# Fewer warm-up matmuls, all at the start, and a new instruction order around them

## The chip, the core and the metric

The kernel runs on one core of a Trainium2 chip. The metric is the device time of one execution in microseconds. The engines are PE (TensorE), DVE (VectorE), ACT (ScalarE), POOL (GpSimd) and SP (SyncE, which here only issues DMAs); each takes its own instructions in order.

## The reference

Two blocks, each behind a layer norm that is modulated by a condition vector `c`, for 2048 tokens of width 512:

```python
mod = (silu(c) @ w_mod).reshape(1, 6, 1, 512)          # sa, ca, ga, sb, cb, gb
h = layernorm(x) * (1 + ca) + sa
x = x + ga * A(h)      # attention: 32 heads of 16, causal, a window of 256 tokens
h = layernorm(x) * (1 + cb) + sb
x = x + gb * B(h)      # layernorm again, then an MLP over the token axis:
                       # u = gelu(h^T @ w1 + b1), y = u @ w2 + b2, transposed back
```

`A` computes `qkv = h @ wqkv`, the scores of each query with the 256 keys up to its own position, their softmax, the weighted sum of the values and the product with `wo`. `w1` is 2048 x 1792, `w2` 1792 x 2048.

## The kernel before

Tokens stand in 16 tiles of 128. Four groups G of four tiles go through the first norm, the transpose (`h1T`, with the features on partitions), the projections to Q, K and V and the attention. Attention is cut into 75 chunks. Chunk i consists of S(i), a group of score matmuls of 32 rows each, four side by side, with 512 columns in each of four PSUM banks; two exps on ACT, a large one over three banks (`pss` to `et`, called EA) and a small one over the fourth (`psb` to `et`, EB); and a multiplication with the mask on DVE. Every few chunks the AV matmuls (`po`) follow, then ln and exp on ACT (`lz`, the reciprocal of the softmax sum) and a multiplication on DVE (`OT`). There is one three-bank tile `pss`, so S(i) waits until EA(i-1) has read it.

Between two score groups PE does other work: the projections of the next group (`pk`, `pq`, `pv`), the output projection (`pa`) of the last one, later the first half of the MLP's first product (`pu`, "partials", from w1 tiles `w1p` that SP loads). After the last chunk come the rest of `pu` and the second product `py`.

The opening (`proj0`, `opening`, lines 609 to 720) makes the first keys and queries. Warm matmuls on a zero tile (`warm`, lines 441 to 455) fill PE early: 16 matmuls of 128x512, two to an operation, into the `pss` tile. `silu` of c goes through a transpose on PE (`st`) and a copy on DVE (`sT`); 32 matmuls of one column (`fm`, output `ps_fm`) make the modulation of the first norm, copied by `fmc` to `modFM`. The first two token tiles are normalized (`xn`), transposed on PE (`tr`, output `psb`) and copied (`cp`) to `h1T`, which is then scaled and shifted with `modFM` (four operations `h1T`). Then come k, k, q, and another k and q, and S(0). The first k waits for `h1T` and for the warm matmuls, which use the same PSUM tile.

The order in which instructions stand on each engine is written out in the kernel. Every piece of work is an `Op`; `ORDER` (line 60) lists them all by number, `CHOSEN` (line 114) says which engine does those that several could do, and `run_schedule` (line 154) emits them in that order. A helper at line 234 keeps every emitted instruction in that program order, so in the profile all of them have line 234 (L234). The tail after the last `gg` operation is a plain loop over 16 output tiles.

Of the kernel before, what the change touches and what calls it, by code (L numbers as in the profile page):

```python
# [15 lines left out]
D = 512  # L16
# [41 lines left out]
E_BUFS = 7  # L58
LOG = None
ORDER = [  # L60
    2, 38, 3, 9, 40, 1, 10, 11, 4, 12, 41, 13, 14, 42, 16, 39, 8, 43, 44, 45, 17, 46, 18, 48, 47, 19, 6, 20, 7, 51,
    50, 49, 5, 52, 0, 53, 54, 56, 55, 57, 70, 58, 71, 126, 72, 75, 127, 73, 59, 76, 80, 60, 123, 81, 74, 128, 130,
    77, 61, 78, 82, 85, 131, 79, 86, 84, 83, 89, 63, 62, 132, 134, 87, 64, 124, 135, 65, 15, 67, 68, 66, 90, 88, 69,
    136, 138, 139, 264, 93, 121, 94, 129, 106, 91, 95, 142, 140, 96, 107, 265, 143, 98, 97, 92, 108, 266, 144, 166,
    111, 167, 267, 109, 99, 145, 268, 168, 100, 170, 112, 171, 110, 146, 133, 147, 113, 151, 137, 148, 174, 172,
    115, 152, 149, 173, 102, 175, 103, 150, 114, 141, 27, 104, 153, 269, 184, 176, 28, 494, 154, 156, 185, 271, 270,
    155, 157, 29, 116, 273, 177, 117, 272, 158, 188, 186, 118, 161, 159, 275, 120, 189, 495, 24, 119, 276, 187, 160,
    190, 198, 496, 101, 25, 199, 274, 724, 21, 22, 169, 162, 105, 200, 26, 202, 163, 23, 30, 203, 31, 497, 178, 191,
    498, 164, 206, 204, 179, 165, 32, 207, 180, 192, 193, 277, 194, 278, 181, 216, 208, 182, 279, 217, 183, 280,
    499, 36, 286, 281, 287, 218, 220, 282, 283, 195, 288, 221, 284, 209, 289, 292, 285, 222, 501, 725, 332, 196,  # L70
    293, 333, 290, 205, 298, 201, 299, 503, 294, 334, 336, 197, 295, 210, 291, 337, 37, 211, 34, 33, 212, 505, 125,
    500, 223, 314, 213, 340, 35, 338, 315, 300, 341, 956, 957, 219, 302, 310, 316, 311, 214, 335, 350, 296, 342,
    224, 312, 225, 351, 726, 226, 313, 301, 233, 215, 339, 352, 354, 504, 234, 727, 355, 297, 304, 235, 305, 728,
    356, 343, 364, 230, 227, 306, 365, 231, 357, 307, 317, 318, 232, 228, 368, 958, 366, 353, 344, 229, 369, 345,
    242, 122, 239, 319, 370, 308, 372, 236, 373, 371, 502, 237, 303, 243, 240, 374, 238, 506, 309, 382, 346, 383,
    241, 321, 320, 244, 322, 358, 384, 245, 386, 359, 347, 387, 323, 959, 246, 360, 375, 328, 348, 396, 388, 329,
    349, 508, 397, 324, 325, 330, 507, 361, 400, 729, 398, 367, 401, 516, 326, 247, 517, 399, 376, 518, 362, 404,
    402, 377, 389, 520, 519, 405, 513, 385, 363, 514, 731, 960, 248, 378, 406, 414, 249, 522, 515, 379, 415, 523,
    255, 327, 390, 391, 524, 380, 331, 732, 418, 416, 392, 381, 250, 419, 526, 509, 525, 510, 403, 521, 393, 407,
    428, 730, 420, 528, 511, 733, 429, 529, 408, 251, 734, 530, 430, 432, 417, 512, 540, 394, 256, 433, 531, 409,  # L80
    421, 541, 252, 410, 253, 434, 436, 411, 395, 437, 735, 542, 534, 257, 547, 527, 736, 412, 254, 446, 438, 548,
    543, 447, 413, 535, 961, 258, 422, 423, 536, 448, 450, 259, 439, 554, 451, 549, 555, 424, 537, 435, 452, 562,
    431, 544, 425, 556, 563, 545, 551, 546, 552, 532, 564, 566, 453, 440, 426, 261, 567, 738, 441, 442, 427, 538,
    449, 443, 737, 570, 568, 550, 454, 455, 444, 565, 571, 456, 445, 553, 463, 464, 533, 569, 457, 580, 572, 460,
    465, 260, 581, 461, 573, 739, 262, 462, 740, 458, 584, 582, 263, 459, 558, 472, 585, 466, 557, 583, 467, 741,
    586, 594, 468, 469, 595, 539, 473, 470, 758, 471, 596, 598, 559, 474, 599, 574, 475, 575, 600, 597, 602, 476,
    560, 576, 603, 759, 587, 743, 760, 744, 604, 612, 601, 577, 746, 613, 745, 747, 605, 588, 589, 477, 578, 748,
    616, 614, 749, 752, 617, 479, 615, 753, 579, 590, 478, 750, 962, 618, 626, 754, 762, 591, 481, 627, 480, 763,
    606, 742, 485, 592, 630, 755, 619, 628, 631, 482, 483, 486, 761, 632, 634, 593, 607, 487, 635, 608, 765, 484,
    751, 766, 609, 764, 963, 644, 636, 488, 645, 620, 621, 767, 622, 489, 633, 646, 648, 772, 610, 629, 561, 649,  # L90
    773, 611, 637, 784, 785, 647, 623, 774, 658, 650, 786, 659, 638, 491, 651, 769, 493, 770, 624, 662, 660, 639,
    771, 490, 663, 640, 625, 652, 492, 653, 654, 641, 768, 666, 664, 964, 642, 667, 965, 643, 966, 661, 665, 756,
    967, 668, 676, 969, 968, 655, 776, 677, 970, 669, 971, 757, 972, 678, 680, 670, 656, 681, 657, 671, 679, 672,
    973, 778, 673, 792, 974, 682, 779, 793, 683, 975, 976, 775, 977, 674, 796, 794, 978, 675, 780, 797, 684, 685,
    979, 782, 686, 795, 798, 800, 787, 690, 781, 687, 799, 801, 691, 693, 692, 694, 688, 810, 802, 788, 689, 695,
    811, 696, 803, 789, 697, 812, 790, 791, 814, 699, 815, 702, 980, 700, 703, 981, 816, 698, 824, 982, 701, 825,
    804, 813, 805, 704, 806, 826, 828, 817, 807, 986, 829, 705, 987, 983, 706, 988, 808, 984, 832, 830, 989, 833,
    809, 818, 831, 819, 827, 820, 990, 834, 842, 821, 991, 835, 843, 707, 992, 993, 777, 994, 844, 846, 822, 836,
    995, 847, 709, 837, 823, 838, 708, 783, 997, 848, 856, 710, 839, 711, 998, 857, 1002, 849, 1003, 712, 1004, 840,
    860, 858, 841, 999, 845, 861, 1005, 1000, 1008, 713, 862, 1001, 864, 1009, 865, 859, 714, 850, 1006, 851, 715,  # L100
    1007, 852, 866, 874, 863, 853, 1010, 875, 716, 1013, 1014, 1011, 854, 878, 876, 855, 1015, 867, 879, 1016, 1012,
    920, 717, 921, 880, 888, 1017, 1019, 922, 889, 1018, 923, 926, 1020, 924, 718, 890, 892, 996, 868, 881, 893,
    719, 869, 925, 870, 985, 1021, 927, 894, 896, 871, 1024, 897, 895, 1022, 891, 1025, 1023, 1026, 928, 720, 906,
    898, 929, 1030, 877, 907, 721, 1027, 899, 1031, 1028, 1032, 722, 872, 910, 908, 873, 882, 723, 883, 909, 911,
    884, 931, 930, 900, 901, 912, 933, 1033, 885, 1042, 1050, 886, 913, 1057, 1034, 932, 902, 914, 903, 915, 887,
    904, 916, 905, 1043, 917, 934, 1051, 918, 1058, 919, 935, 1071, 938, 936, 939, 1035, 940, 941, 942, 944, 1036,
    1064, 943, 1065, 1085, 945, 1037, 1078, 937, 946, 1038, 947, 1086, 1039, 948, 1072, 1052, 1040, 949, 1092, 951,
    1044, 1093, 950, 1029, 1087, 1066, 952, 1079, 1041, 1059, 953, 1094, 1080, 954, 955, 1073, 1045, 1046, 1067,
    1047, 1053, 1060, 1048, 1054, 1081, 1095, 1061, 1055, 1099, 1049, 1062, 1074, 1068, 1088, 1056, 1113, 1069,
    1075, 1100, 1106, 1063, 1076, 1082, 1107, 1108, 1089, 1083, 1109, 1120, 1077, 1070, 1127, 1096, 1101, 1090,  # L110
    1114, 1084, 1097, 1102, 1115, 1103, 1116, 1128, 1110, 1104, 1129, 1091, 1134, 1117, 1111, 1121, 1105, 1122,
    1098, 1123, 1118, 1135, 1124, 1136, 1112, 1130, 1125, 1119, 1137, 1131, 1138, 1132, 1139, 1133, 1126, 1140,
]
CHOSEN = {
    "ACT": [
        48, 50, 72, 74, 95, 1017, 1034, 1039,
    ],
    "DVE": [
        47, 49, 51, 52, 66, 69, 77, 79, 82, 84, 87, 91, 97, 100, 104, 108, 110, 113, 115, 118, 120, 248, 250, 252, 254,
        277, 278, 281, 285, 288, 294, 300, 306, 312, 316, 319, 323, 326, 330, 478, 480, 482, 484, 507, 508, 511, 515,  # L120
        518, 524, 530, 536, 542, 546, 549, 553, 556, 560, 708, 710, 737, 738, 741, 745, 748, 754, 760, 764, 767, 771,
        774, 780, 786, 790, 968, 973, 979, 984, 990, 995, 1001, 1006, 1012, 1023, 1028,
    ],
    "POOL": [
        712, 714,
    ],
}
BATCH = True
XT_AFTER = -0.7
W1_AFTER = 2.0  # L130
AV_POS = 0.2
LZ_POS = 0.0
M_POS = -0.5
# [60 lines left out]
def kernel(  # L194
# [116 lines left out]
    warm = modw.tile([P, D], BF, name="warm")  # L311
# [135 lines left out]
    def e_par(e):  # L447
        for par in range(2):
            ve.tensor_reduce(
                out=mask_par[:, par : par + 1], in_=ident_v[:, :, par, :], axis=mybir.AxisListType.XY, op=ALU.add,  # L450
            )

    parity = op("par", "DVE", 0.33, e_par, pos=-30, ready=2.2)
    warms = [op("warm", "PE", 0.86 if i < 4 else 0.43, lambda e, i=i: e_warm(e, 2, i == 0), pos=-7, cls="D", ready=1.4 if i < 4 else 4.8)
             for i in range(8)]

    def e_stps(e):
        box["st"] = bank([P, ND], BF, "st_ps")
# [3 lines left out]
            ready=2.8, pos=-20)  # L462
# [24 lines left out]
    fms = []  # L487
# [2 lines left out]
                      alloc=None if n else "od", ready=MOD_READY[n]))  # L490
    o_fm = op("fmc", "DVE", 0.25, e_fmc, deps=fms[-1:], pos=-12)
    fms[0].frees = [o_fm]


    def dense(name, pieces, emit, deps, pos, cls="D", alloc=None, ready=0.0):
# [858 lines left out]
```

## Time and profile before

| | |
|---|---|
| median of 3 runs | 257.99 us (256.64 to 258.8) |
| profiled execution, its own time | 258.61 us |
| its span, first to last instruction | 256.8 us |
| PE busy | 241.1 us (94%) |
| DVE, ACT, POOL busy | 200.6 (78%), 179.9 (70%), 133.0 us (52%) |
| mean granted clock of PE | 0.993 |
| first k matmul, first score group, first large exp | 10.49, 12.45, 12.89 us |
| first `pu` matmul on the chain that ended last | 125.68 us |
| first `py` matmul | 204.7 us |

A time in the profile counts from the start of the span. Busy time of PE includes the time that a matmul is in the pipeline, so a full PE need not run at its peak. "Granted clock" is the share of the full clock that PE was given. Names such as `pss<-QT,KT` are output and inputs of an instruction.

### The profile page before, as it was taken

The page shows a single profiled execution, that of the slowest core. Times are in us where ns is not written, and L with a number is a line of the kernel's source. Part 1 is how long each engine was busy: PE and PEld are TensorE (multiplying, and loading weights), DVE is VectorE, ACT ScalarE, POOL GpSimd, SP SyncE. Part 2 cuts the span into 40 slices and gives each one's busy share as a digit, 9 for nine tenths or more (in the row PEclk, how much of TensorE's full clock was granted, in tenths as well). Part 3 has the DMA queues.
Part 4 walks back from the last instruction along what each step waited for, and adds up shares of the span by engine and source line. Part 5 has one row for each costly group of instructions (what it writes and reads, how often), then busy time and mean ns, then how long its engine had stood idle before and what let it go on. Part 6 is the DMA issues. An engine that isn't in the chain of part 4 may idle for free.

```text
span 256.8 us, 8133 instructions
## 1 busy us (share of the span) xinstructions
PE 241.1 (94%) x3427; PEld 122.2 (48%) x3427; DVE 200.6 (78%) x392; ACT 179.9 (70%) x255; POOL 133.0 (52%) x237
## 2 busy tenths in 40 slices
PE   7988989899998999979999999999999999999994
PEld 2665635444443454434545454446444444444443
DVE  4589999998899999998658879799869864444442
ACT  4399999999999999998999999998138510000000
POOL 8288977999999897896914389190000000000000
PEclk9999999999999999989999999999999999999999
DMA  7998360246254400060030003351899601111111
GB/s 222 326 349 252 12 80 3 42 114 159 61 120 60 116 3 3 9 182 0 5 92 14 3 3 84 106 142 37 326 332 387 232 22 41 58 48 41 41 43 41
DMA packets 41341, 27.02 MB, mean 105 GB/s; under 512 B 11992, under 2 KB 37208, under 8 KB 41304
## 3 DMA queue, kind: packets, MB, share of 16 engines
q1 hardware_dynamic: 41008, 25.97, 36.2%
q8 instruction: 27, 0.44, 0.7%
q10 hardware_dynamic: 296, 0.53, 0.6%
q14 instruction: 10, 0.08, 0.1%
HBM read 22.03 MB, written 2.10 MB: 94 GB/s over the span
## 4 chain that ended last, share of the span: by engine, by line
PE 61%; POOL 12%; DVE 10%; ACT 8%; issue 4%; DMA 3%; SPq 0%; DVEq 0%; POOLq 0%
PE pu L234 20%; PE py L234 19%; PE po L234 7%; ACT et L234 6%; PE pss L234 6%; POOL VT L234 4%; PE pa L234 3%; DVE et L234 3%; POOL xn L234 3%; POOL KT L234 2%; PE pk L234 2%; DMA w1p<-in_B_w_dram 2%; PE pv L234 2%; ACT lz L234 1%; DVE vb L234 1%
## 5 line engine op out<-in xcount | busy, mean ns | idle before, releaser
L234 ACT ACTIVATE et<-pss 128x1536 bf16<-128x1536 f32 x75 | 110.8, 1477 | 3.3 <-PE psb L234 1.7
L234 PE MATMUL pu<-hb,w1p 128*128 128x512 bf16 x224 | 52.6, 380 | 0.0
L234 DVE TENSOR_TENSOR et<-et,maskt 128x1024 bf16<-128x1024 bf16 (+2 forms) x79 | 48.5, 628 | 2.7 <-ACT et L234 2.6
L234 PE MATMUL py<-guT,w2r 128*128 128x512 bf16 (+1 forms) x238 | 48.7, 366 | 0.5 <-DVE otile L234 0.5
L234 ACT ACTIVATE et<-psb 128x512 bf16<-128x512 f32 x75 | 46.9, 626 | 0.0
L234 PE MATMUL pss<-QT,KT 32*128 32x64 bf16 (+3 forms) x720 | 30.0, 232 | 6.6 <-ACT et L234 5.0
L234 PEld LDWEIGHTS <-w2r 128*128 128x128 bf16 x238 | 23.3, 98 | 26.0 <-issue 0.7
L234 PE MATMUL po<-et,VT 128*32 128x64 bf16 (+3 forms) x960 | 32.3, 237 | 1.0 <-DVE kb L234 0.6
L234 PEld LDWEIGHTS <-w1p 128*128 128x128 bf16 x224 | 20.4, 98 | 25.0 <-issue 2.5
L234 PE MATMUL po<-et,ones_bd 128*32 128x256 bf16 (+3 forms) x624 | 32.0, 271 | 0.0
L234 POOL TENSOR_SCALAR KT<-kb,mask_par 128x512 bf16<-128x512 bf16 (+1 forms) x38 | 27.4, 732 | 7.2 <-ACT kb L234 5.8
L234 DVE TENSOR_TENSOR otile<-py,xr 128x512 bf16<-128x512 f32 (+1 forms) x17 | 11.2, 660 | 25.3 <-PE py L234 25.2
L234 PEld LDWEIGHTS <-KT 32*128 32x128 bf16 x960 | 15.8, 93 | 31.1 <-issue 28.9
L234 PE MATMUL psb<-QT,KT 32*128 32x64 bf16 (+3 forms) x240 | 29.5, 232 | 0.0
L234 PEld LDWEIGHTS <-VT 128*32 128x32 bf16 x960 | 19.6, 97 | 12.9 <-issue 10.7
L234 POOL TENSOR_SCALAR xn<-x,rs,nm 128x512 bf16<-128x512 bf16 x24 | 22.8, 951 | 1.4 <-DVE h L234 0.5
L234 DVE BATCH_NORM_STATS2 st<-x 128x6 f32<-128x512 bf16 x32 | 21.4, 682 | 2.2 <-DMA x<-in_A_x_dram 2.1
L234 PE MATMUL pk<-h1T,wqkv 128*128 128x256 bf16 (+2 forms) x108 | 21.3, 326 | 0.6 <-DVE vb L234 0.5
L234 PEld LDWEIGHTS <-wqkv 128*128 128x128 bf16 x164 | 13.8, 99 | 13.4 <-issue 6.0
L234 DVE TENSOR_TENSOR OT<-po,lz 128x256 bf16<-128x256 f32 x32 | 13.3, 416 | 8.2 <-ACT lz L234 8.2
L234 PE MATMUL pv<-wqkv,h1T 128*64 128x256 bf16 (+1 forms) x112 | 17.2, 321 | 0.4 <-DVE OT L234 0.4
L234 PE MATMUL pa<-wod,OT 128*128 128x512 bf16 x64 | 17.0, 380 | 0.4 <-DVE kb L234 0.2
(99 smaller groups left out, 324.1 us busy)
## 6 DMA issues: line engine op xcount, KB each, us to landing
w1p<-in_B_w_dram SPq DMA_DIRECT2D x14, 512.0 KB, 5.0
w2r<-in_B_w_dram SPq DMA_DIRECT2D x14, 512.0 KB, 7.8
x<-in_A_x_dram SPq DMA_DIRECT2D x16, 128.0 KB, 5.2
wmod<-in_w_mod_dram SPq DMA_DIRECT2D x4, 512.0 KB, 8.6
out_dram<-otile SPq DMA_DIRECT2D x15, 128.0 KB, 1.7
wqkv<-in_A_wqkv_dram SPq DMA_DIRECT2D x4, 256.0 KB, 4.9
vs<-vb SPq DMA_DIRECT2D x24, 32.0 KB, 3.0
wmod<-in_w_mod_dram ACTq DMA_DIRECT2D x2, 256.0 KB, 3.7
```

What stands on the lines that cost most here:

```text
L234: ins = call(*args, **kwargs)
```

## The change

Six warm operations (12 matmuls) take the place of eight (16 matmuls), all with the same early time in the table, and the second `fm` operation now depends on all of them. In the new `ORDER` all 12 warm matmuls stand first on PE, ahead of the transpose of silu; before, 8 stood there, 2 between the first two `fm` operations and 6 between the last `fm` and the first k. All four `fm` operations now follow the transposes `tr`, where two stood before or between them. `CHOSEN` moves five operations to another engine: one of the two `cp` copies from DVE to ACT, one query copy of the opening and one key copy after chunk 3 from ACT to DVE, and of two late `part` copies one each way.

```diff
-    warms = [op("warm", "PE", 0.86 if i < 4 else 0.43, lambda e, i=i: e_warm(e, 2, i == 0), pos=-7, cls="D", ready=1.4 if i < 4 else 4.8)
-             for i in range(8)]
+    warms = [op("warm", "PE", 0.86, lambda e, i=i: e_warm(e, 2, i == 0), pos=-7, cls="D", ready=1.4) for i in range(6)]
...
     fms[0].frees = [o_fm]
+    fms[1].deps += warms
```

`ORDER` and the DVE list of `CHOSEN` are replaced as a whole (the numbers of all later operations fall by two); their first lines show how:

```diff
 ORDER = [
-    2, 38, 3, 9, 40, 1, 10, 11, 4, 12, 41, 13, 14, 42, 16, 39, 8, 43, 44, 45, 17, 46, 18, 48, 47, 19, 6, 20, 7, 51,
...
+    5, 36, 0, 4, 7, 38, 2, 8, 9, 3, 10, 39, 6, 40, 37, 1, 41, 42, 11, 43, 12, 44, 14, 46, 15, 16, 45, 17, 18, 49,
...
 CHOSEN = {
     "ACT": [
-        48, 50, 72, 74, 95, 1017, 1034, 1039,
+        45, 46, 48, 70, 1010, 1032, 1037,
```

Past the opening the two orders differ by exchanges of near neighbours. On PE they are these where whole groups change segment (a segment is what stands after S(i) and before S(i+1)); AV numbers count the AV groups:

| segment | before | after |
|---|---|---|
| S(43) | v, v, AV47, AV48 | v, v, AV47 |
| S(44) | v, v, AV49 | AV48, q |
| S(45) | q, q, AV50 | q, AV49 |
| S(46) | nothing | v, v, AV50 |
| S(47) | AV51, AV52, k, k | AV51, k, AV52, k |

On SP the first `w1p` load stood behind one of the four DMA transposes of token group 2 and now stands behind three. On DVE the query copy of the third key-query group in the opening (`qe3`) now stands behind the two `xn` operations that it stood ahead of. On POOL one `hb` operation moves from segment 36 to 44.

## The prediction

> **What bounds the kernel now.** I read the page's busy shares and slices first, then the stretches, then the timeline around the two places that the stretches single out.
>
> ```profile
> span 256.8 us, 8133 instructions
> ...
> PE 241.1 (94%) x3427; PEld 122.2 (48%) x3427; DVE 200.6 (78%) x392; ACT 179.9 (70%) x255; POOL 133.0 (52%) x237
> ...
> PE   7988989899998999979999999999999999999994
> ...
> ACT  4399999999999999998999999998138510000000
> POOL 8288977999999897896914389190000000000000
> PEclk9999999999999999989999999999999999999999
> ```
>
> ACT is full from slice 2 to 27, PE from slice 19 to the end; one slice (the 19th, around 116 us) has a lower clock, and the slice before it the lowest PE digit of the middle. Until 118 us PE mostly follows ACT: score group S(i) writes the one three-bank tile that the large exp of chunk i-1 reads, and of PE's waits between 12 and 120 us the largest sum, 5.0 us in 9 waits, is for that exp. From 130 to 174 us both are full (43.97 and 43.05 of 44 us), after that PE alone. So a microsecond lost or won before 118 us, on ACT's sequence or on PE's, reaches the end.
>
> The stretches (us; busy time of PE with its count, PEld, DVE, ACT, POOL; then the granted clock, DMA share, GB/s):
>
> ```profile
> 0.50:3.90 3.40, 2.63 (x7) 0.96 (x8) 1.13 (x4) 2.21 (x4) 2.91 (x12) 1.00 0.59 140
> 3.90:7.30 3.40, 2.95 (x29) 1.48 (x28) 1.92 (x7) 0.50 (x2) 3.33 (x9) 1.00 1.06 369
> 7.30:10.70 3.40, 3.40 (x28) 1.75 (x27) 1.77 (x8) 1.20 (x2) 0.76 (x4) 1.00 1.13 308
> ...
> 20.90:24.30 3.40, 2.73 (x45) 1.57 (x45) 3.40 (x9) 3.40 (x6) 2.70 (x6) 1.00 0.90 284
> 109.70:113.10 3.40, 1.61 (x36) 0.75 (x34) 3.33 (x7) 3.40 (x6) 3.40 (x4) 1.00 0.69 188
> 113.10:116.50 3.40, 3.27 (x56) 1.77 (x55) 3.37 (x7) 2.85 (x5) 2.62 (x5) 0.50 0.56 157
> ```
>
> PE ran at half clock for one stretch of 3.4 us, 113.1 to 116.5, right after a stretch in which it was busy 1.61 of 3.40 us (47%); 2.73 of 3.40 (80%) at 20.9 did not bring that about. Cut into steps of 3.4 us from there, the start shows the reverse. The clock column says 1.00 there too, but the spacing of the matmuls says otherwise, and I go by spacing:
>
> ```profile
> 1.27 3.59 PE L234 MATMUL pss<-warm 128*128 128x512 bf16 x8 [1.27 <-DVE warm L312]
> ...
> 7.98 2.72 PE L234 MATMUL pss<-warm 128*128 128x512 bf16 x6
> 10.49 0.49 PE L234 MATMUL pss<-h1T,wqkv 128*128 128x128 bf16 x4
> ...
> 11.48 1.04 PE L234 MATMUL pk<-h1T,wqkv 128*128 128x256 bf16 x8
> ...
> 113.22 0.29 PE L234 MATMUL pss<-QT,KT 32*128 32x128 bf16 x3 [1.72 <-ACT et L234]
> ...
> 117.23 1.45 ACT L234 ACTIVATE et<-pss 128x1536 bf16<-128x1536 f32 x1 [1.06 <-PE psb L234]
> ```
>
> The warm matmuls follow each other at 0.427 us (their weight loads start at 1.68, 2.10, 2.53 ...), the last six too; in the tail 512 columns take 0.216 (the chain has 106 u matmuls in 22.88 us), and the 256-column matmuls at 11.48 start 0.108 apart. So the clock rose between 10.1 and 11, after the stretch 7.3 to 10.7 in which PE was full, and not after the stretches that were 77% and 87% full. The last two lines are the cost in the middle: PE idles 1.72 us before S47 because nothing stands between S46 and S47 in its order, the clock halves, and ACT then waits 0.21 + 1.06 us.
>
> **The change, part by part.** (1) *The warm matmuls.* Four of 16 go; twelve now run in a row from 1.27 us, to 1.27 + 12 x 0.427 = 6.39. The transpose of silu moves from 4.80 to 4.80 + 4 x 0.427 = 6.51, its copy sT from 5.24 to about 6.8 (0.13 long, behind the second xn, which ends at 6.67). The xn transposes run in that gap: 6.55 to 6.98, and 6.98 to 7.41, at 0.107 each. All 32 ps_fm matmuls follow at 0.04 each (16 in 0.63), 7.45 to 8.75, result about 8.85 where before it came at 8.12. The two copies of the transposes now both stand on ACT (0.60 each, 7.75 to 8.95), still ahead of what needs them. modFM and the h1T operations shift by 0.73: DVE's three end at 9.36 + 0.73 = 10.1 and k can start at 10.2. Before, k waited for the last six warm matmuls until 10.49. Net: 0.3 us earlier, not the 1.7 us of four matmuls, because what was hidden behind the warm block (ps_fm to h1T) is now itself the path.
>
> (2) *What the warm block also did.* Before, it filled 7.3 to 10.7. In the new order PE has there the rest of the transposes (0.15), ps_fm (1.3), nothing from 8.9 to 10.2, and 0.5 of k: about 2.0 of 3.4 us, 59%. That is far from the full stretch that raised the clock, and between the 47% that lowered it and the 80% that did not. The bounds: full clock at 10.2, or half clock to 14.1. I take half, since of ps_fm's 1.3 us nearly all is weight loads of one-column matmuls. Then k, k, q and the next k and q (512 + 512 + 1024 + 2048 columns) take 3.4 instead of 1.7 us: S0 at about 13.6 instead of 12.45, and the first exp 1.2 to 1.5 late.
>
> (3) *Moves off ACT.* One query copy (0.38, at 14.24) leaves ACT between the first exps and one key copy (0.38, at 21.12) after the fourth. Their share in the step is 0.27 and at most 0.2 us; DVE takes them, and there the third query copy now stands behind the two xn (1.97 us), which puts 0.42 ahead of vb and so of the pt transposes that S3 follows. I net these at -0.2, bounds -0.5 and +0.4. At the fourth exp the opening is +1.3 - 0.2 = +1.1 us; with a full clock it would be -0.3 - 0.2 = -0.5.
>
> (4) *The hole at 111.5 us.* The new order has two v matmul groups (4 x 512 columns, 1.04 us) and an AV group between S46 and S47, taken from the two segments before. The stretch would be busy some 2.6 of 3.4 us (77%), near the 80% that kept the clock. Gain: the 0.21 + 1.06 us that ACT waited, 1.3 us; bounds 0 (the hole only moves to the thinner segments) and 1.4 (S48 at 115.4, the end of exp 47, instead of 116.78).
>
> (5) *The rest of the order.* Counted in columns, PE's projection, wo and MLP work before each S(i) is the old sum less the four warm matmuls in nearly all of the 75 segments; the differences are of one group (0.43 us) and are made good one or two segments later. On SP the first w1 load stands behind three of the four transposes of token group 2 instead of one; its first reader comes at 125.7 us, and the load lands in 5 us, so that costs nothing, and if that cover were gone, 5 us. On POOL one hb operation (about 0.9 us) moves eight segments later, also well ahead of that reader; the zeroing of VT and the KT splits change places by one. In the tail the u groups change places within an order that leaves PE full. I put all this at 0, bounds -0.8 (the ACT waits that remain are about that) and +1.5 (the longest single wait of PE for ACT, 1.7, is what one badly placed group can cost).
>
> Sum, against the profiled execution of 258.61 us (span 256.8 and 1.8 around it): 258.6 + 1.1 - 1.3 + 0 = **258.4 us**. That execution is 0.6 above the median of 257.99; it holds the half-clock stretch at 113, which other executions need not, and a clock that rose just when k began.
>
> [...]
>
> **The rivals.** *A, the clock holds.* The twelve warm matmuls raise it at about 7.3 (PE full from 3.9 to 7.3) and 59% is enough to keep it. For: 59% lies above 47%. Against: warm matmuls that filled 77% and 87% of a stretch raised nothing. Time: 258.6 - 0.5 - 1.3 = 256.8.
> *B, the clock falls twice: slower.* After the opening at half clock PE meets the segments S44 and S45, each lighter by 0.43 us of v and q matmuls than before, so the idle of 1.7 us is only spread and a stretch there still falls below what keeps the clock. It decides if the busy share is nearer 47% than 80%. Price: the 1.3 us are not won, and the half-clock stretch, nearly full of needed work (3.27 of 3.40), costs up to half of it, 1.6, instead of 1.3 beside idle. With +1.1 to +1.5 at the start: 258.6 + 1.3 + 0.3 = 260.2, and 261.7 where a misplaced group adds its 1.5.
> *C, the change does nothing for the path.* The opening's loss is taken up: the fourth exp had a wait of 0.48 and PE waited 0.41 to 0.60 for ACT at S2, S5 and S6. For: those rows. Against: ACT has no idle from 23 to 52 us, so what is late at the fourth exp stays late. With the hole gone: 258.6 - 1.3 = 257.3.
>
> **How the numbers follow.** Forecast 0.42, A 0.20, B 0.25, C 0.13. The range 256.0 to 261.7 goes from A with the -0.8 of part 5 to B with its misplaced group. A measurement of this kernel tells about 1% (2.6 us) from no change. Faster than 255.4 would need A and more than part 5's lower bound: 0.09. Slower than 260.6 takes B's upper half (0.13) or the forecast with part 5's upper bound and more against it (0.15): 0.28. Within 1%: 0.63.
>
> **What would show it.** In the changed profile: 0.427 us between all twelve warm matmuls or a drop in the last of them; k at about 10.2; its 256-column matmuls at 0.21 (half clock) or 0.108; a clock record of 0.50 near 10.7 to 14.1 or none; the first exp at about 14.2 against 12.89; no 1.72 us gap before S47 and no half clock at 113 us. I am wrong if the first exp starts before 12.9, or if ACT or PE shows a new wait over 1.5 us between 30 and 120 us.

## Result, and the profile after

The changed kernel takes 258.84 us (median of 20 executions, 257.1 to 260.46) against 256.65 us for the kernel before (20 executions taken with them, 255.32 to 259.17). The ratio is 1.0085, with an interval of 1.0058 to 1.0112: slower by 0.85%, or 2.2 us, and within the 1% that I had called no change. The profiled execution of the changed kernel took 258.43 us, 0.2 less than the one of before. So the two profiles alone show almost nothing; the profile of before is of one of its slower executions. The page of the changed kernel:

```profile
span 256.4 us, 8125 instructions
...
PE 238.8 (93%) x3423; PEld 121.1 (47%) x3423; DVE 201.7 (79%) x393; ACT 179.7 (70%) x254; POOL 134.2 (52%) x237
...
PE   7779989899988899888999999999999999999994
...
ACT  4688999999999999999999998997236610000000
POOL 8487988989999985997943369290000000000000
PEclk9998999999999999999999999999999999999999
```

PE is busy 2.3 us less, DVE 1.1 us more. The low clock has gone from the 19th slice to the fourth, and in the second to fourth slice ACT has 6, 8 and 8 tenths where it had 3, 9 and 9: it starts earlier and is then less full. Four stretches of the changed kernel (columns as in the prediction) say when the clock did what:

```profile
4.50:7.95 3.45, 2.73 (x46) 1.70 (x44) 1.51 (x8) 1.66 (x5) 3.29 (x12) 1.00 1.07 352
7.95:11.36 3.41, 2.58 (x36) 2.13 (x37) 1.98 (x7) 1.77 (x5) 0.07 (x1) 1.00 1.13 316
...
14.78:18.19 3.41, 2.00 (x42) 1.31 (x40) 3.41 (x8) 2.79 (x4) 2.73 (x5) 1.00 1.10 349
18.19:21.60 3.41, 3.41 (x37) 2.06 (x30) 2.88 (x9) 2.75 (x3) 2.08 (x4) 0.50 1.10 348
```

The clock rose at 4.54, while the warm matmuls ran, and stayed up through the idle before k. Up to that moment PE has done the same in both orders: the first eight warm matmuls alone last from 1.27 to 4.69 at 0.427 us each. It fell at 18.19, after a stretch in which PE was busy 2.00 of 3.41 us. The timeline of the changed kernel in the opening, and its S46, where the longest wait of PE around the old hole now is:

```profile
1.27 4.36 PE L234 MATMUL pss<-warm 128*128 128x512 bf16 x12 [1.27 <-DVE warm L312]
6.56 0.94 PE L234 MATMUL ps_fm<-sT,wmod 128*128 128x1 bf16 x32
...
8.79 0.38 PE L234 MATMUL pss<-h1T,wqkv 128*128 128x128 bf16 x4 [1.29 <-DVE h1T L234]
...
9.66 1.04 PE L234 MATMUL pk<-h1T,wqkv 128*128 128x256 bf16 x8
...
11.08 1.45 ACT L234 ACTIVATE et<-pss 128x1536 bf16<-128x1536 f32 x1
...
110.72 0.26 PE L234 MATMUL pss<-QT,KT 32*128 32x192 bf16 x3 [0.64 <-ACT et L234]
```

Twelve warm matmuls take 4.36 us instead of 5.12, because the last of them run at the full clock. The first k starts at 8.79 instead of 10.49 and the first large exp at 11.08 instead of 12.89. The wait of 1.72 us before S47 is gone. Both places that the change works on are better in this pair of profiles, the first exp by 1.8 us and the step from exp 47 to 48 by 1.1, and yet the spans differ by 0.4 us. The rest went elsewhere. The starts of the large exps cut both spans into parts. Two more executions, one of each kernel, in which the clock rose early (at 3.93 and 4.71 us) and never fell, show the two orders alone (us; y2_before and y3_after are told of below):

| part, from start of large exp to start of large exp | before, profiled | after, profiled | difference | y2_before | y3_after | difference | ACT idle, y2 / y3 |
|---|---|---|---|---|---|---|---|
| span's start to 0 | 12.89 | 11.08 | -1.81 | 11.06 | 11.08 | +0.02 | |
| 0 to 5 | 10.94 | 12.01 | +1.07 | 10.45 | 11.29 | +0.84 | 0.04 / 1.22 |
| 5 to 29 | 51.50 | 51.16 | -0.34 | 51.61 | 51.12 | -0.49 | 0.42 / 0.14 |
| 29 to 37 | 17.54 | 18.71 | +1.17 | 17.53 | 18.68 | +1.15 | 0.22 / 1.09 |
| 37 to 47 | 21.01 | 20.46 | -0.55 | 20.81 | 20.44 | -0.37 | 0.12 / 0.02 |
| 47 to 50 | 7.55 | 7.26 | -0.29 | 6.90 | 7.25 | +0.35 | 0.25 / 0.61 |
| 50 to 67 | 36.42 | 36.91 | +0.49 | 36.42 | 36.90 | +0.48 | 0.60 / 1.10 |
| 67 to the end | 98.95 | 98.8 | -0.1 | 98.9 | 99.0 | +0.1 | |
| span | 256.8 | 256.4 | -0.4 | 253.7 | 255.8 | +2.1 | |

At the full clock the new order is 2.1 us longer. The two copies that leave ACT are seen (its work from exp 0 to exp 5 is 10.08 instead of 10.41 us), but ACT's idle grows by more, in four parts. The profile of before had carried two losses that were its own: a clock that rose at 10.7 (the 1.81) and the fall at 113 (part of the 7.55).

### The profile page after: what moved, and what is told of

Same layout as the page of the kernel before. It is cut to its first block, busy times and chain, and to the rows that moved or that the text cites. A ratio compares the mean times of both kernels' runs of the same rounds, so it can differ in the third digit from the quotient of the medians.

```text
span 256.4 us, 8125 instructions
## 1 busy us (share of the span) xinstructions
PE 238.8 (93%) x3423; PEld 121.1 (47%) x3423; DVE 201.7 (79%) x393; ACT 179.7 (70%) x254; POOL 134.2 (52%) x237
## 4 chain that ended last, share of the span: by engine, by line
PE 60%; DVE 20%; ACT 10%; issue 5%; DMA 4%; SPq 0%; DVEq 0%
PE py L234 19%; PE pu L234 18%; ACT et L234 8%; PE po L234 8%; PE pss L234 5%; DVE et L234 5%; DVE h L234 4%; PE pa L234 3%; PE pk L234 3%; DVE st L234 2%; DVE kb L234 2%; DMA wmod<-in_w_mod_dram 2%; ACT lz L234 2%; DVE vb L234 2%; DMA x<-in_A_x_dram 2%
## 5 line engine op out<-in xcount | busy, mean ns | idle before, releaser
L234 DVE TENSOR_TENSOR et<-et,maskt 128x1024 bf16<-128x1024 bf16 (+2 forms) x79 | 46.9, 609 | 2.1 <-ACT et L234 1.9
L234 PE MATMUL po<-et,ones_bd 128*32 128x256 bf16 (+3 forms) x624 | 31.3, 268 | 0.0
L234 POOL TENSOR_SCALAR xn<-x,rs,nm 128x512 bf16<-128x512 bf16 x24 | 24.9, 1040 | 2.8 <-DVE h L234 1.9
L234 PEld LDWEIGHTS <-VT 128*32 128x32 bf16 x960 | 18.9, 96 | 14.5 <-issue 12.4
L234 PE MATMUL pk<-h1T,wqkv 128*128 128x256 bf16 (+2 forms) x108 | 22.2, 335 | 1.7 <-DVE kb L234 1.2
L234 PEld LDWEIGHTS <-wqkv 128*128 128x128 bf16 x164 | 14.2, 101 | 15.6 <-issue 7.4
L234 PE MATMUL pa<-wod,OT 128*128 128x512 bf16 x64 | 16.3, 380 | 0.0
## 6 DMA issues: line engine op xcount, KB each, us to landing
wqkv<-in_A_wqkv_dram SPq DMA_DIRECT2D x4, 256.0 KB, 5.7
wmod<-in_w_mod_dram ACTq DMA_DIRECT2D x2, 256.0 KB, 4.0
```

The source lines that it names most:

```text
L234: ins = call(*args, **kwargs)
```

## Experiments

Where the clock matters I name the time of its steps. Each ratio is to runs of the kernel before on the same chip. The runs x1 to x4 were on one chip, x5 to x8 on a second, x9 and y1 to y3 on a third; where times of two groups are compared, the ratios are the safer measure. What the warm matmuls write is never read, so kernels that add some or leave some out compute the same.

### The kernel before once more: x1_before

No edit.

> The kernel before once more, unchanged, for its spans and granted clocks over many executions (the earlier ones have times alone). Both theories expect a median of 256.7 us. The theory that the clock's falls make the spread expects executions to lie in groups by the mean granted clock: 1.00 (no stretch at half clock) shortest, 0.993 (one stretch of 3.4 us) about 1.0 to 1.3 us longer, 0.986 another step; the profiled one before had one such stretch, at 113 us, and 256.8 us of span, so those without should have about 255.4. If the clock does not make the spread, spans differ as much within a group as between groups.

256.77 against 256.24 us, ratio 1.0013 (0.9989 to 1.0037). The profile has its rise at 10.50, no fall, a span of 256.0 us and the first exp at 12.70. Sorting executions by their mean granted clock went wrong: those at 1.000 were at 256.0, longer than those at 0.993 (nine of twelve, 254.4 to 255.3). A late rise does not show in the mean: this profile has 1.000 with its rise at 10.50. Over 84 executions of the kernel before, from all three chips, 15 have spans of 253.4 to 253.9 us at 0.998 or more, 42 have 254.0 to 255.4 at 0.993 (one half-clock stretch), 11 have 255.6 to 256.0 at 1.000, and 10 have 256.5 to 257.2 at 0.986 to 0.993 (six lie between or above these). The profile shown before, with 256.8, was in the last group.

### The opening alone, and the rest alone: x2_opening, x3_rest

x2_opening takes the warm matmuls, `fm`, the second `cp` on ACT and the order of the new kernel up to S0, and the old order after it; x3_rest is the reverse.

```diff
 # x2_opening, against the kernel before; ORDER as in the new kernel up to S0
-    warms = [op("warm", "PE", 0.86 if i < 4 else 0.43, lambda e, i=i: e_warm(e, 2, i == 0), pos=-7, cls="D", ready=1.4 if i < 4 else 4.8)
-             for i in range(8)]
+    warms = [op("warm", "PE", 0.86, lambda e, i=i: e_warm(e, 2, i == 0), pos=-7, cls="D", ready=1.4) for i in range(6)]
...
+    fms[1].deps += warms
```

> One part alone: the new kernel's instructions up to the first score group (12 warm matmuls at the start, ps_fm after the transposes, both copies on ACT), and from there the old order. Theory R (the loss sits in the order after the first score group, the opening itself gains): faster than before by 0.5 to 1.5 us, 255.2 to 256.2, the first large exp at about 11.1 us instead of 12.9 and most of these 1.8 us kept to the end. Theory O (the opening loses, because it leaves PE thin until 18 us and the clock then falls): slower than before by 1 to 2 us, 257.7 to 258.7, like the whole change.

> The other part alone: the old opening with its 16 warm matmuls up to the first score group, and from there the new order. Theory R: slower than before by 2.5 to 3.5 us, 259.2 to 260.2, more than the whole change; in its profile PE waits for DVE around chunks 34, 36, 50 and 67, as in the changed kernel. Theory O: like before within 0.5 us, 256.2 to 257.2.

x2_opening: 258.44 us, ratio 1.0072 (1.0038 to 1.0105). x3_rest: 257.21 us, ratio 1.0064 (1.0038 to 1.0091). Each half costs something by itself. The time of x2_opening is what theory O expected; x3_rest is at the upper end of theory O and 2 us below theory R, though the waits that theory R named are there. The halves sum to 1.36%, the whole is 0.85%; why they don't add up is open. x2_opening still has the old hole at 111 us. Its stretches:

```profile
5.23:8.64 3.41, 2.44 (x45) 1.67 (x44) 1.59 (x8) 1.91 (x5) 2.58 (x12) 1.00 1.08 333
8.64:12.05 3.41, 3.06 (x19) 2.44 (x19) 2.03 (x7) 0.66 (x3) 0.00 (x0) 0.50 1.13 326
```

Here the same opening lost the clock at 8.64, just before k. Eight k matmuls that took 1.04 us in the changed kernel took 1.73, and the first exp came at 12.75 instead of 11.08:

```profile
10.65 1.73 PE L234 MATMUL pk<-h1T,wqkv 128*128 128x256 bf16 x8
```

So the opening has two outcomes, and the good one only equals the old opening with an early rise (11.06), while the bad one equals the old opening with a late rise (12.70).

x3_rest has the waits of the second half of the story. Two of them, in the timeline of ACT:

```profile
121.15 1.45 ACT L234 ACTIVATE et<-pss 128x1536 bf16<-128x1536 f32 x1 [0.62 <-PE psb L234]
...
158.05 1.45 ACT L234 ACTIVATE et<-pss 128x1536 bf16<-128x1536 f32 x1 [0.74 <-PE psb L234]
```

They are at exps 50 and 67, as in the changed kernel, with the old opening ahead of them: the order of the rest makes them, not a late start.

### Only eight warm matmuls: x4_eight

```diff
 # against x2_opening
-    warms = [op("warm", "PE", 0.86, lambda e, i=i: e_warm(e, 2, i == 0), pos=-7, cls="D", ready=1.4) for i in range(6)]
+    warms = [op("warm", "PE", 0.86, lambda e, i=i: e_warm(e, 2 if 0 < i < 5 else 0, i == 0), pos=-7, cls="D", ready=1.4) for i in range(6)]
```

> As the kernel with the new opening alone, but with 8 warm matmuls at the start instead of 12 (four are left out; they compute nothing that is used). If 12 in a row are what raises the clock early (theory C): the clock is not up when the first k begins, k and q of the opening take 0.21 us a 256-column matmul instead of 0.108, and the first exp comes 0.5 to 1.5 us later than with 12; time 0.5 to 1.5 us above that kernel. If the number does not matter and the block is merely on the path of the silu transpose (rival D): 0 to 0.8 us below it, as the transpose moves ahead by up to 0.85 to 1.7 us.

259.03 us, ratio 1.0122 (1.0097 to 1.0147), 0.6 us above x2_opening, as theory C expected; the two intervals overlap. The clock rose only at 13.58; S0's exp came at 13.33. A stretch of x4_eight:

```profile
6.75:10.17 3.42, 2.13 (x44) 2.11 (x43) 1.46 (x7) 1.69 (x3) 1.13 (x7) 1.00 1.15 310
```

After eight matmuls the clock did not rise behind the two stretches before k (2.37 and 2.13 us of 3.41), and k and q run at half clock. Eight in a row are not always too few: with the old opening, which also starts with eight, it rose at 3.93, 4.21 and 4.22 us in y2_before, x3_rest and y1_before, and at 10.50 and 10.70 in the two other profiles. With twelve in a row it rose at 4.54 and 4.71 in the changed kernel and y3_after, and at 5.23, 4.23 and 5.17 in x2_opening, x5_fill and x8_undo. As far as so few profiles go, what the four more buy is an early clock in more of the executions.

### Filling the gap before k: x5_fill, x6_open_fill

```diff
 # x5_fill against the changed kernel, x6_open_fill against x2_opening
-        fms.append(op("fm", "PE", 0.27, lambda e, n=n: e_fm(n), deps=[o6] + fms[-1:], pos=-12.4 + 0.1 * n, cls="D",
+        fms.append(op("fm", "PE", 0.27, lambda e, n=n: (e_fm(n), n == ND - 1 and [e_warm(e, 2, False) for _ in range(2)]), deps=[o6] + fms[-1:], pos=-12.4 + 0.1 * n, cls="D",
```

Four warm matmuls follow the last `fm` matmul, in the time in which PE waits for `h1T`.

> The changed kernel with four more warm matmuls between the last ps_fm matmul and the first k, where PE sits idle while modFM and h1T are made (7.5 to 8.8 us in the changed kernel's profile). Theory F (the new opening loses because that idle stretch lets the clock fall just before k, q and the first score groups, in most executions): the profile has no half-clock stretch that begins between 7 and 11 us, the first large exp stands at 11.1 to 11.5 us, and the time is 1 to 2 us below the changed kernel's, 256.8 to 257.8, of which a fall around 18 us may take back 1. Rival G (the clock's phase has nothing to do with it; the four matmuls merely stand before k): 0 to 1 us slower than the changed kernel, 258.8 to 259.8.

> The same four matmuls in the kernel that has the new opening and then the old order (258.4 us, against 256.2 before on that chip). Theory F: 1.5 to 3 us below that kernel, so faster than before by 0 to 1.5 us, 255 to 256.5. Rival G: 258.4 to 259.4.

x5_fill: 257.57 us, ratio 1.0027 (0.9991 to 1.0062), 1.3 us below the changed kernel (by the ratios 0.58%, with intervals that just touch). Its executions were without a fall ten times in twelve, at spans of 255.2 to 256.1; of the changed kernel's twenty, three were, at 255.4 to 256.0. So the fill does not make an undisturbed execution shorter (the first exp is at 11.08 in both); it takes falls away. x6_open_fill: 256.58 us, ratio 0.9978 (0.994 to 1.0015), 1.9 us below x2_opening. With the fill, the opening alone can't be told from the kernel before. What x5_fill still loses to x6_open_fill, 1.0 us, lies in the order after S0.

Two stretches of x5_fill also show what a busy share does not tell:

```profile
7.64:11.06 3.42, 3.02 (x36) 1.99 (x36) 2.02 (x8) 1.74 (x5) 0.24 (x2) 1.00 1.14 315
...
14.47:17.88 3.41, 2.01 (x36) 1.30 (x32) 3.41 (x7) 3.09 (x4) 2.73 (x5) 1.00 1.10 350
```

The first holds the fill (3.02 us against 2.58 in the changed kernel). After the second, 59% busy, the clock stayed up, while after an equally busy stretch of the changed kernel (2.00 at 14.78) it fell.

### Both kernels at the full clock: y1_before, y2_before, y3_after

No edit.

> The kernel before once more, for a profile of its commonest execution (spans of 254.4 to 255.1 with a mean clock of 0.993; the two profiles so far, 256.8 and 256.0, lie above it). Theory F: the clock rises before 8 us, stays up through the last six warm matmuls or falls for one stretch, and the first exp comes at 11.5 to 13.0 us; the other 1.5 us to the two profiles come from there and from chunks 3 to 5, not from the order, whose steps between chunks 9 and 45 are the same to 0.1 us. Rival E (the executions differ by other things than the clock): the steps between chunks 9 and 45 differ too.

> The same again, since the place of the clock's steps differs from one execution to the next: another of its executions, by theory F with the same steps of the exps from chunk 9 to 45 and with a first exp that follows from when the clock rose.

> The changed kernel once more, for a second execution. Theory F: where the clock's step ends between 8 and 9 us it falls there (PE is busy about 72% of the stretch before), the first exp comes at 12.6 us; where it ends near 8 us (79% busy) it holds, the first exp comes at 11.1 us and the clock falls around 18 us. In both the waits at chunks 34, 36, 50 and 67 are 0.3, 0.3, 0.6 and 0.7 us. Rival E: those waits move or vanish with the clock's steps.

255.23, 255.44 and 257.51 us, spans 253.5, 253.7 and 255.8. That y1 would be of the commonest kind and that y3 would fall at 18 were both wrong; all three had a rise at 3.9 to 4.7 and no fall, which makes y2 and y3 the best pair for the two orders (the table above). In y1_before the last six warm matmuls take 1.46 us, 2.72 in the profile shown before, and k starts at 8.46 instead of 10.49, with the same instructions:

```profile
7.16 1.46 PE L234 MATMUL pss<-warm 128*128 128x512 bf16 x6
```

That steps between the same chunks don't differ from one execution to another held nearly: exps 9 to 45 took 76.84, 76.75 and 76.71 us in x1, y1 and y2, and 76.60 in the profile shown before, where 0.1 had been expected to be the most. The timelines of the third chunk, first y2_before, then y3_after:

```profile
14.26 0.82 DVE L234 TENSOR_SCALAR xn<-x,mv,rs 128x512 bf16<-128x512 bf16 x2
15.01 0.67 DVE L234 CAST vb<-pv 128x512 bf16<-128x512 f32 x1
15.37 0.95 POOL L234 MEMSET VT<- 128x1024 bf16 x1
15.41 0.70 PE L234 MATMUL pt<-identity,xn 128*128 128x128 bf16 x8
...
17.46 1.45 ACT L234 ACTIVATE et<-pss 128x1536 bf16<-128x1536 f32 x1
```

```profile
14.22 1.97 DVE L234 TENSOR_SCALAR xn<-x,mv,rs 128x512 bf16<-128x512 bf16 x2
14.61 0.95 POOL L234 MEMSET VT<- 128x1024 bf16 x1
...
16.12 0.40 DVE L234 CAST QT<-pk 128x256 bf16<-128x256 f32 x1
16.44 0.68 DVE L234 CAST vb<-pv 128x512 bf16<-128x512 f32 x1
16.57 0.38 PE L234 MATMUL pt<-identity,xn 128*128 128x128 bf16 x4 [0.88 <-DVE QT L234]
...
18.49 1.45 ACT L234 ACTIVATE et<-pss 128x1536 bf16<-128x1536 f32 x1 [0.82 <-PE psb L234]
```

In the new order POOL zeroes VT while DVE makes `xn`: the first of the two `xn` takes 1.49 us, from 14.22 to 15.71, and ends just after the zeroing does (15.57). The query copy and `vb` stand behind it, PE's transposes wait 0.88 us for the copy, and the exp of chunk 3 waits 0.82 us. In y2_before the pair is over at 15.08, before the zeroing begins. The old order is not always spared: in the profile shown before, the second `xn`, from 16.36, meets the zeroing (16.72 to 17.67) and takes 1.45 us. Chunk 67 of y3_after shows the same on another pair:

```profile
152.26 1.56 POOL L234 TENSOR_TENSOR h<-xn,bc_cb 128x512 bf16<-128x512 bf16 x1
152.74 1.37 DVE L234 TENSOR_TENSOR h<-xn,bc_cb 128x512 bf16<-128x512 bf16 x1
...
154.14 1.26 DVE L234 TENSOR_TENSOR h<-h,bc_sb 128x512 bf16<-128x512 bf16 x1
...
156.76 1.45 ACT L234 ACTIVATE et<-pss 128x1536 bf16<-128x1536 f32 x1 [0.74 <-PE psb L234]
```

Both engines work on `h` at one time. On DVE the two operations take 1.37 and 1.26 us. The `OT` behind them is late, PE's next `pu` waits for it, and the exp waits 0.74. The same work in y1_before:

```profile
149.54 0.42 DVE L234 TENSOR_TENSOR h<-xn,bc_cb 128x512 bf16<-128x512 bf16 x1
149.99 0.80 DVE L234 TENSOR_TENSOR h<-h,bc_sb 128x512 bf16<-128x512 bf16 x1
150.60 1.20 POOL L234 TENSOR_TENSOR h<-xn,bc_cb 128x512 bf16<-128x512 bf16 x1
150.71 1.63 DVE L234 TENSOR_TENSOR et<-et,maskt 128x1024 bf16<-128x1024 bf16 x1
```

There POOL begins its two only 0.2 us before DVE's are over, and these take 0.42 and 0.80. What meets POOL is the mask multiplication behind them (1.63 us; the 43 of this shape in the profile shown before take 0.75 on average), and the exp of chunk 67 waits only 0.23. In both of these places DVE is the queue that got longer; PE and ACT only pass it on.

### The old order in two places: x8_undo

The changed kernel with the old order from S29 to S38 and from S62 to S71. The first places of `ORDER` that differ:

```diff
...
-    389, 513, 378, 249, 416, 414, 405, 523, 507, 417, 524, 397, 390, 253,
+    389, 513, 378, 249, 957, 397, 958, 253, 730, 416, 414, 390, 379, 417,
...
```

> The changed kernel with two stretches of its order undone: the old order from the 29th to the 38th score group and from the 62nd to the 71st. Theory R (each of the waits at chunks 34, 36 and 67 comes from DVE's new order there): the waits of 0.32, 0.34 and 0.74 us before exps 34, 36 and 67 are gone from the profile, and the time falls by 1.0 to 1.6 us, to 257.2 to 257.8. Rival P (they come from being earlier after the opening, and appear elsewhere): the waits move to other chunks and the time stays within 0.4 us of 258.8.

257.12 us, ratio 1.0012 (0.9978 to 1.0046): 1.7 us less than the changed kernel, by the ratios 0.73%, with intervals that don't touch. The waits at exps 36 and 67 went (0.34 to 0, 0.74 to 0.23, as in the kernel before), and the two `h` of DVE take 0.42 and 0.80 again; exps 29 to 37 took 18.03 us (old 17.54, new 18.71). The wait at exp 34, which was expected to go, stayed at 0.30, there is one of 0.35 at exp 31, behind the seam of new and old order, and at 50, in the new part, one of 0.47. Two stretches of old order give back most of what the change cost, although this profile has the half-clock stretch just before k, with its first exp at 12.62. So a large part of the cost is the order after S0, in those places. That this 0.73% and the 0.58% of the fill sum to more than the 0.85% of the change is no contradiction: the kernel before has falls of its own.

### Two attempts at a better version: x7_hybrid_fill, x9_candidate

x7_hybrid_fill is x5_fill with the new order up to S29 and from S42 to S48, and the old one elsewhere. x9_candidate is x6_open_fill with one q group (761 in the list) and AV50 (604) moved from ahead of S46 (628) to behind it, into the old hole:

```diff
...
-    625, 478, 761, 604, 740, 483, 590, 628, 753,
+    625, 478, 740, 483, 590, 628, 761, 604, 753,
...
```

> A candidate: the new opening with the four matmuls; the new order up to the 29th score group and between the 42nd and the 48th, the old order elsewhere. By the exps' starts in the profiles the new order is 0.97 us ahead of the old at chunk 29 and gives 1.14 back by chunk 37, 0.36 around chunk 50 and 0.48 at chunk 67; the old one has an idle stretch at chunk 47 that can halve the clock. Theory R with F: 1 to 1.5 us below the kernel with the new opening, the four matmuls and the old order, so 254 to 255.5. If the parts can't be put together (the moved groups meet other neighbours and wait): like that kernel or slower, 255.5 to 257.

> A candidate: the new opening with the four extra warm matmuls, the old order after the first score group, and in it one q matmul pair (0.43 us) and one AV group moved from before to after the 46th score group, where PE otherwise idles 1.72 us. Theory F (falls of the clock are what is left to win): no half-clock stretch near 113 us in any execution; executions of the kernel without that move had spans of 253.6 to 254.8 without a fall and 254.6 to 255.8 with one, so the median falls by 0.3 to 0.6 us to 256.0 to 256.3, and against before the ratio is 0.993 to 0.997. Rival M (the moved q pair and AV group come too late for what follows them): a new wait of ACT or PE at chunks 47 to 50, and no gain, 256.5 to 257.5.

x7_hybrid_fill: 256.53 us, ratio 0.9993 (0.9958 to 1.0028). It fell short of what was expected and can't be told from the kernel before: its profile has new waits of 0.81 at exp 50 and 0.35 at 31, each a few chunks behind a seam. x9_candidate: 256.41 us, ratio 1.0001 (0.9972 to 1.0031). In the profile the clock still fell, at 111.48, after a stretch with 1.65 us of PE work; none had been expected, but by the mean clock three of its twelve executions had one (five of twelve in x6_open_fill). The wait moved ahead of S46, as its timeline shows:

```profile
109.40 0.26 PE L234 MATMUL pss<-QT,KT 32*128 32x192 bf16 x3 [1.17 <-ACT et L234]
```

None of these versions beats the kernel before by more than the interval.

## Why the prediction was right, and where it was wrong

Forecast 258.4, measured 258.84, on the side that was called within 1%. The time is near partly by luck. Up to the fourth exp I forecast +1.1 us, and the pair of profiles has -1.35; for the hole -1.3, and it has -1.06; for everything else 0, and it has +2.0 (part of that the fall at 18.19). Two errors, of 2.4 and 2.0 us, nearly cancel, and the base moved as well.

- **The base.** I summed against one execution of 256.8 us span and named the half-clock stretch and the late rise as things that others need not have. They mostly don't: 61 of 84 spans were below 255.5. Against that execution I forecast 0.2 us less; against the 256.65 that the kernel before has in 20 executions, the same 258.4 is 1.75 more. The 1.3 us of part 4 were a gain over a loss that comes only at times.
- **Part 1, the warm matmuls.** The chain was right in its steps (ps_fm to `h1T` is the path, PE waits 1.29 us for `h1T`), and wrong in the clock: k came at 8.79 and not at 10.2.
- **Part 2, the clock.** Wrong. I took a rise after 14 us and a first exp near 14.2; it was 11.08 in the profile, and 12.75 or 12.62 in x2_opening and x8_undo, which have the same opening. I had said that a first exp before 12.9 would prove me wrong, and it did. The step that failed is the choice of the stretch: I measured the new order against 7.3 to 10.7, where the clock of before had risen, and found 59% there, as if no rise could come earlier. That place belonged to one execution and not to the order: with the same old opening the clock rose at 3.93 and 4.22 in y2_before and y1_before, with first exps at 11.06 and 10.75. The old opening with an early rise is as early as the new one, so the 1.8 us that the pair of profiles shows at the first exp belongs to the two executions and is not a gain of the new opening. Whether the clock then lives until k is a near thing: the stretch before was 72% (2.44) and 68% (2.33) busy where it was lost, 76% (2.58) and 79% (2.73) where it stayed. Where it was lost, the price, 12.75 - 11.08 = 1.7 us, is close to my 1.2 to 1.5. Rival A was right that the clock is up before k and stays up in the profiled execution; its rise at 7.3 and its 256.8 us did not come. The rise came at 4.54, 3.27 us after the first warm matmul. The clock fell behind stretches in which PE's longest wait was 0.89 us (before 18.19 in the changed kernel) and 1.72 us (at 111 in the kernel before), and stayed up through the 1.29 us before k.
- **Part 3, the copies.** Taken at -0.2 up to the fourth exp, measured +1.0 (exp 0 to 3: 7.41 us in y3_after, 6.40 in y2_before), of which 0.84 is left at exp 5. The bound of +0.4 was too small. The query copy behind the two `xn` was named, with its 0.42; the zeroing of VT beside `xn`, which I had in part 5 as a change of place that costs nothing, makes the pair 1.97 us long and is what turns that into 0.82 of ACT's wait. In the profile of before the pair took 1.97 as well, beside the zeroing; so the row that I used already held the collision, and I didn't see that the old kernel is free of it in executions such as y1 and y2. About half of the +1.0 comes with the opening alone: exp 0 to 3 takes 6.88 and 6.89 us in x6_open_fill and x9_candidate, which have the old order after S0.
- **Part 4, the hole.** Right for the pair of profiles: the wait of 1.72 is gone and the step from exp 47 to 48 is 2.29 instead of 3.35 us. But it is a gain only over executions that fall there. At the full clock the old hole costs ACT 0.17 at exp 48, and the new order loses more than that at exp 50 (0.61). There PE's k group waits 0.73 us for a `kb` copy that stands behind a statistics operation on DVE.
- **Part 5, the rest of the order.** Taken at 0, with bounds of -0.8 and +1.5. From exp 5 on, the table has +1.15, +0.35, +0.48 and +0.1 against -0.49 and -0.37: +1.2, inside the bounds but not near the middle. I had counted PE's columns per segment, which hardly change, and not DVE's order, where copies that free PSUM tiles now stand behind longer work. No single gap of PE between 30 and 120 us passes 0.73; it is a sum of waits of ACT of 0.3 to 0.7 at exps 32, 34, 36, 50 and 67.
- **Rival B** (two losses of the clock) happened in three executions of twenty, at spans of 258.1 to 258.3. Rival C was half true in a way that I had not meant: an opening that is better by 1.8 us in the profile is taken back by exp 37, where the two profiles stand at 92.87 and 92.96.

What settles the size: the order at the full clock makes 2.1 us, about the whole of the 2.2 measured, and the executions without a fall bear the two profiles out (253.4 to 253.9 before, 15 of them; 255.4 to 256.0 after, three). Falls of the clock cost both kernels, the old one behind its hole, the new one before k or at 18 us; the fill suggests that those of the new one are worth about 1.3, by a comparison across two series of runs. Not settled is why the clock is lost after one stretch that is 59% busy and kept after another. Nor was a kernel run with both the fill and the old order of x8_undo.

## What to carry to other kernels

When an order is replaced, compare the queue of every engine and not only the one that is full: ask of each copy that frees a PSUM tile what now stands ahead of it, and what another engine does at the same time (here one `xn` on DVE took 1.49 us beside POOL's zeroing, two took 0.82 us ahead of it). A block of warm matmuls that seems only to start the clock may also be what keeps it (with four in the gap before k, ten executions of twelve were without a fall, without them three of twenty); look at how full PE is in the stretch before the first dense work, here 3.4 us long. And take the base of a sum from several executions, with the time of the first exp and the steps of the clock in each.

## What the runs showed of the hardware

- **The clock's steps lay on a grid.** In the pair of profiles the times between steps were multiples of 3.413 us (13.653 from 4.54 to 18.19 in the changed kernel, 102.4 from 10.70 to 113.10 in the kernel before, 3.413 for the half-clock stretch of each), and the grid lay differently in each execution: the changed kernel rose at 4.54 and at 4.71. That is how one opening had two outcomes: with the rise at 4.54 and 4.71 the stretches before k held 2.58 to 2.75 us of PE work and kept the clock, with 5.23 and 5.17 they held 2.44 and 2.33 and lost it. The old hole shows the same: its 1.72 us of idle are in y1_before too (before 110.75), and the clock stayed up, with 2.44 us of PE work from 110.04 to 113.45, against 1.61 from 109.70 to 113.10 in the profile shown before. The grid is not all: x3_rest rose at 4.21 and y1_before at 4.22, with the same opening, but in x3_rest the next stretch held 2.01 us (4.21 to 7.62), in y1_before 2.93 (cut from 4.43 to 7.84), and only in x3_rest did the clock fall, at 7.62.
- **Falls came without a long gap.** Cut along the grid from the rise to 205 us, the pair of profiles has one stretch each that lost the clock, with 47% of PE busy in the kernel before (1.61 us) and 59% in the changed kernel (2.00); all their other stretches had 72% or more and kept it. In other runs it was lost behind 45% (1.53 us, from 111.04 in x2_opening), 48% (1.65, from 108.07 in x9_candidate), 59% (2.01, from 4.21 in x3_rest), 68% (2.33, from 5.17 in x8_undo) and 72% (2.44, from 5.23 in x2_opening), and kept behind 59% (2.01, from 14.47 in x5_fill and from 14.95 in y3_after) and 72% (2.44, from 110.04 in y1_before). So the busy share alone does not decide. One fall was 3.41 us at half clock, and cost about 0.7 us behind the old hole (part 47 to 50: 7.55 against 6.90; the groups at 254.0 to 255.4 and at 253.4 to 253.9 have medians 0.9 apart) and 1.5 to 1.7 where it hits k (12.62 and 12.75 against 11.08).
- **DVE was slower beside some of POOL's work.** One `xn` took 1.49 us when it met the zeroing of VT (the changed kernel), against 0.82 for two of them ahead of it (y2_before, 14.26 to 15.08); `h` took 1.37 us beside POOL's `h` (y3_after) and 0.42 ahead of it (y1_before). Overlap alone did not do it: the two `xn` of y2_before ran beside POOL's `KT` (13.45 to 15.43), the `h` of y1_before beside POOL's `xn` (149.34 to 150.52), and in y3_after a mask multiplication of 0.67 us at 152.14 overlaps POOL's `h` from 152.26. What makes the difference, no run here shows.
